# Units of 512, 384 and 256 tokens, batch 0 transposed on TensorE, and the later loads on the GpSimd queue, in an attention and channel-mix kernel

## The chip, the cores and the metric

One core of one Trainium2 chip. The time is the device time of a run in microseconds (us). Most executions of one kernel agree within 0.3%; a run over 1.5% above the fastest of its kernel is called slow here, and only fast runs are compared. Before: 229.57 us, median of 3 (228.76 to 230.91); with a fourth run in the comparison below, 229.41.

Engines: PE is TensorE's matmul, PEld its weight load, DVE is VectorE, ACT is ScalarE, POOL is GpSimd, SP is SyncE. A trailing q ("SPq") is an engine's sequencer. SyncE only issues DMAs here.

## The reference, cut to what matters

Eight batches, eight heads, 576 tokens, head size 64. The attention is linear, so it costs little; the channel mix after it has the arithmetic.

```python
q_s = softmax(q, axis=-1)          # over the 64 of a head
k_s = softmax(k, axis=2)           # over the 576 tokens
kv  = einsum('bhsd,bhse->bhde', k_s, v)
x   = einsum('bhsd,bhde->bhse', q_s, kv)      # -> (8, 576, 512)

x_prev = x shifted by one token
xk = mu_k * x + (1 - mu_k) * x_prev
xr = mu_r * x + (1 - mu_r) * x_prev
k  = maximum(xk @ w_k, 0)          # 512 -> 1024
v  = k * k @ w_v                   # 1024 -> 512
out = sigmoid(xr @ w_r) * v
```

## The kernel before

Each batch is done in two groups of four heads. `attention(b, g)` is a generator: ACT makes exp(q), exp(k) and a bf16 copy of v; VectorE normalises q into `qs`; PE makes `kvp`; a DMA transpose turns `qs` into `qt`; PE multiplies it by `w` into `xp`; ACT and VectorE make `xb`, `xd`, and the mixed `xk` and `xr`. `unit(n)` is the channel mix of 384 tokens: 8 `kfp` groups of four matmuls (`xk @ w_k`), then for each 128 tokens one `rp` (`xr @ w_r`) and one `vp` (the squares times `w_v`). The program interleaves steps of the attention of a later batch with the pieces of a unit.

```python
    def emit_load(b: int, g: int, gate=None):
        t = ldpool.tile([128, 3, 2, J * D], F32, tag="raw", name="raw")
        for i, src in enumerate((q, k, v)):
            ap = ...                                  # 128 partitions x 2 rows of 2304 bytes
            ld = nc.sync.dma_start(out=t[:, i, :, :], in_=ap)
            after(ld, gate)                           # a semaphore wait, where given
            gate = None
        ...
    # in attention():
        qt = apool.tile([128, J, 128], BF16, tag="qt", name="qt")
        nc.sync.dma_start_transpose(out=qt[:], in_=qs[:].rearrange("p j c -> p (j c)"))
    # in unit(): each 128 tokens of the result are two stores
                nc.sync.dma_start(out=dst, in_=ot[64 * i:64 * i + 64, :])
    # weights: ten DMAs with a cast to bf16, all issued by nc.gpsimd, behind batch 0's first v load
    wdone = emit_weights(first)
    ...
    emit_load(1, 0, wdone[3])         # batch 1's loads wait for weights
    emit_load(1, 1, wdone[7])
    ...
                if b + 1 < B:         # later: the loads of the next batch
                    emit_load(b + 1, g, wdone[-1] if b == 1 and g == 0 else None)
                yield from attention(b, g)
```

So SyncE issues every load of q, k and v, every transpose and every store; GpSimd issues only weights, the last of them at 17 us.

The softmax here doesn't subtract the row's maximum and nothing guards it: scores larger than these inputs give would overflow.

## Time and profile before

| what | before |
|---|---|
| time, median | 229.57 us |
| profiled span | 228.1 us |
| PE busy | 182.5 us (80%) |
| VectorE busy | 160.1 us (70%) |
| first long run of `kfp` | 42.3 us |

PE's 45.6 us of idle time (228.1 less 182.5) lie mostly in front of 42 us. The prediction shows those lines. Two more views. The first is of the tile `qt` (duration of the issue in ns as min/median/max, first and last start in us, then the time from issue to landing):

```profile
L189 SPq DMA_TRANSPOSE qt<-qs x16: 1273/1475/10114, 8.8 to 147.6; - x16
...
DMA to landing us min/median/max: 3.2/3.8/16.5
```

Fourteen of sixteen transposes behave alike, and the two of batch 0 took up to 16.5 us. The second is the queues (packets, MB, share of 16 engines' span); q1 carries what SyncE issues, q0 what GpSimd issues:

```profile
q1 hardware_dynamic: 37760, 42.48, 66.8%
q0 software_dynamic: 2208, 2.62, 6.7%
```

### The profile page before, as it was taken

The page shows a single profiled execution, that of the slowest core. Times are in us where ns is not written, and L with a number is a line of the kernel's source. Part 1 is how long each engine was busy: PE and PEld are TensorE (multiplying, and loading weights), DVE is VectorE, ACT ScalarE, POOL GpSimd, SP SyncE. Part 2 cuts the span into 40 slices and gives each one's busy share as a digit, 9 for nine tenths or more (in the row PEclk, how much of TensorE's full clock was granted, in tenths as well). Part 3 has the DMA queues.
Part 4 walks back from the last instruction along what each step waited for, and adds up shares of the span by engine and source line. Part 5 has one row for each costly group of instructions (what it writes and reads, how often), then busy time and mean ns, then how long its engine had stood idle before and what let it go on. Part 6 is the DMA issues. An engine that isn't in the chain of part 4 may idle for free.

```text
span 228.1 us, 3352 instructions
## 1 busy us (share of the span) xinstructions
PE 182.5 (80%) x1153; PEld 92.8 (41%) x1169; DVE 160.1 (70%) x367; ACT 136.0 (60%) x213; POOL 7.1 (3%) x16
## 2 busy tenths in 40 slices
PE   0100055599989989979999999999999999999991
PEld 0100032254543534434544545545545454554540
DVE  0550077899989999799999999995867843343521
ACT  4544048699597886697685994946437254352720
POOL 2360000000000000000000000000000000000000
PEclk9999999599999999999999999999999999999999
DMA  6999999999799999999899899444041140414114
GB/s 222 362 318 207 195 314 393 259 334 285 171 303 295 247 318 232 279 293 275 282 264 313 248 277 275 92 93 98 3 92 46 40 101 1 111 26 95 46 46 95
DMA packets 40009, 45.32 MB, mean 199 GB/s; under 512 B 21048, under 2 KB 22584, under 8 KB 39992
## 3 DMA queue, kind: packets, MB, share of 16 engines
q1 hardware_dynamic: 37760, 42.48, 66.8%
q0 software_dynamic: 2208, 2.62, 6.7%
q8 instruction: 9, 0.15, 0.3%
q14 instruction: 8, 0.07, 0.1%
q10 hardware_dynamic: 24, 0.00, 0.0%
HBM read 33.56 MB, written 9.44 MB: 189 GB/s over the span
## 4 chain that ended last, share of the span: by engine, by line
PE 53%; DVE 18%; DMA 14%; SPq 7%; ACT 3%; issue 2%; DVEq 0%
PE vp L241 21%; PE kfp L223 19%; PE rp L234 10%; DMA raw<-in_q_dram 8%; SPq L189 5%; DMA raw<-in_k_dram 4%; DVE qs L169 3%; DVE rsum L165 3%; PE xp L194 2%; DVE xm L209 2%; DMA qt<-qs 2%; PE kvp L177 2%; DVE xd L203 2%; ACT eqk L157 2%; DVE xk L211 1%
## 5 line engine op out<-in xcount | busy, mean ns | idle before, releaser
L223 PE MATMUL kfp<-xk,wk_bf 128*128 128x384 bf16 x384 | 71.2, 336 | 7.0 <-DVE xk L211 6.4
L227 ACT ACTIVATE rel<-kfp 128x384 bf16<-128x384 f32 x96 | 45.9, 498 | 24.3 <-PE kfp L223 22.5
L223 PEld LDWEIGHTS <-wk_bf 128*128 128x128 bf16 x384 | 36.9, 100 | 34.8 <-issue 10.6
L157 ACT ACTIVATE eqk<-raw 128x1152 bf16<-128x1152 f32 x32 | 37.1, 1167 | 13.6 <-DMA raw<-in_k_dram 6.6
L244 DVE SCALAR_TENSOR_TENSOR ot<-th,vp 128x512 f32<-128x512 f32 x36 | 24.7, 685 | 23.9 <-PE vp L241 20.8
L237 ACT ACTIVATE th<-rp 128x512 f32<-128x512 f32 x36 | 21.6, 601 | 27.6 <-PE rp L234 27.1
L234 PE MATMUL rp<-wr_bf,xr 128*128 128x512 bf16 x132 | 36.5, 379 | 0.6
L194 PE MATMUL xp<-qt,w 128*128 128x512 bf16 x64 | 13.4, 306 | 18.3 <-DMA qt<-qs 17.0
L165 DVE TENSOR_REDUCE rsum<-eqk 128x18 f32<-128x1152 bf16 x16 | 21.4, 1339 | 6.8 <-ACT eqk L157 6.8
L169 DVE TENSOR_TENSOR qs<-eqk,rrec 128x1152 bf16<-128x1152 bf16 x16 | 21.7, 1354 | 0.2
L209 DVE TENSOR_SCALAR xm<-xd,mu 128x576 bf16<-128x576 bf16 x64 | 20.7, 367 | 0.1
L234 PEld LDWEIGHTS <-xr 128*128 128x128 bf16 x144 | 13.4, 98 | 14.2
L177 PEld LDWEIGHTS <-eqk 64*128 64x128 bf16 x288 | 9.4, 99 | 17.5 <-issue 9.7
L194 PEld LDWEIGHTS <-w 128*128 128x128 bf16 x64 | 5.8, 103 | 25.6 <-issue 15.5
L177 PE MATMUL kvp<-vv_100,eqk 64*128 64x129 bf16 x108 | 4.9, 232 | 10.4 <-ACT vv_100 L161 10.4
L197 ACT CAST xb_102<-xp 128x576 bf16<-128x576 f32 x12 | 7.6, 647 | 7.8 <-PE xp L194 7.8
L200 DVE COPY xb_102<-xb_102 128x126 bf16<-128x126 bf16 x6 | 1.2, 194 | 15.2 <-ACT xb_102 L197 15.2
L184 DVE SCALAR_TENSOR_TENSOR w<-kvp,rz,mask 128x128 bf16<-128x128 f32 x32 | 9.7, 342 | 0.2
L197 ACT CAST xb_110<-xp 128x576 bf16<-128x576 f32 x10 | 6.4, 639 | 4.6 <-PE xp L194 4.5
L161 ACT CAST vv_100<-raw 128x1152 bf16<-128x1152 f32 x6 | 7.0, 1167 | 1.5 <-DMA raw<-in_v_dram 1.5
L241 PE MATMUL vp<-wv_bf,k_961 128*128 128x512 bf16 x24 | 6.0, 380 | 1.7 <-DVE k_961 L229 1.7
L161 ACT CAST vv_108<-raw 128x1152 bf16<-128x1152 f32 x5 | 5.8, 1161 | 2.3 <-DMA raw<-in_v_dram 2.3
(75 smaller groups left out, 198.2 us busy)
## 6 DMA issues: line engine op xcount, KB each, us to landing
raw<-in_q_dram SPq DMA_DIRECT2D x16, 576.0 KB, 5.6
raw<-in_k_dram SPq DMA_DIRECT2D x16, 576.0 KB, 5.4
raw<-in_v_dram SPq DMA_DIRECT2D x16, 576.0 KB, 8.3
out_dram<-ot SPq DMA_DIRECT2D x72, 128.0 KB, 2.5
wk_bf<-in_moe_w_k_dram POOLq DMA_DIRECT2D x4, 256.0 KB, 7.6
wv_bf<-in_moe_w_v_dram POOLq DMA_DIRECT2D x2, 512.0 KB, 14.5
wr_bf<-in_moe_w_r_dram POOLq DMA_DIRECT2D x4, 128.0 KB, 11.1
qt<-qs SPq DMA_TRANSPOSE x16, 3.8
```

The costliest lines, as they stand in the source:

```text
L157: nc.scalar.activation(out=eqk[:, i, :, :, :], in_=t[:, i, :, :].rearrange("p u (j d) -> p j u d", d=D), func=ACT.Exp)
L165: nc.vector.reduce_sum(out=rsum[:], in_=eq, axis=AX.X)
L169: nc.vector.tensor_tensor(out=qs[:].rearrange("p j (u d) -> p (j u) d", u=2), in0=eq, in1=rrec[:, :, None].to_broadcast((128, 2 * J, D)), ...
L177: nc.tensor.matmul(kvp[:, hf, 0:129], lhsT=eqk[r, 1, j, :, :].rearrange("p u d -> p (u d)"), rhs=vv[r, j, 0:129], start=(j == 0), stop=(j ...
L194: nc.tensor.matmul(xp[:, 64 * c:64 * e], lhsT=w[:, hf, :], rhs=qt[:, c:e, 64 * hf:64 * hf + 64], start=True, stop=True)
L209: nc.vector.tensor_scalar(out=xm[:, hf, :], in0=xd[:, hf, :], scalar1=mu[:, c:c + 1], scalar2=None, op0=ALU.mult)
L223: nc.tensor.matmul(kfp[:, 0:U], lhsT=wk_bf[:, ct, fc * 128:(fc + 1) * 128], rhs=xk[:, ct, c0:c0 + U], start=(ct == 0), stop=(ct == CT - 1))
L227: nc.scalar.activation(out=rel[:], in_=kfp[:, 0:U], func=ACT.Relu, scale=HALF_ROOT)
L234: nc.tensor.matmul(rp[:], lhsT=xr[:, ct, c0 + 128 * m:c0 + 128 * m + 128], rhs=wr_bf[:, ct, :], start=(ct == 0), stop=(ct == CT - 1))
L237: nc.scalar.activation(out=th[:], in_=rp[:], func=ACT.Tanh, scale=0.5)
L241: nc.tensor.matmul(vp[:], lhsT=k2[:, ft, 128 * m:128 * m + 128], rhs=wv_bf[:, ft, :], start=(ft == 0), stop=(ft == FT - 1))
L244: nc.vector.scalar_tensor_tensor(out=ot[:], in0=th[:], scalar=1.0, in1=vp[:], op0=ALU.add, op1=ALU.mult)
```

## The change

Its intent: start the channel mix earlier (no DMA transpose for batch 0), spread the attention's work evenly over the units, and keep the loads from waiting behind transposes by giving them a queue of their own. The gates that held batch 1's and batch 2's loads until weights had landed go with it. The diff, cut to its core:

```diff
-    U = 384
-    NU = B * S // U
+    UNITS = ((0, 512), (512, 384), (896, 256))
...
-    def emit_load(b: int, g: int, gate=None):
+    def emit_load(b: int, g: int, queue):
...
-            ld = nc.sync.dma_start(out=t[:, i, :, :], in_=ap)
-            after(ld, gate)
-            gate = None
+            ld.append(queue.dma_start(out=t[:, i, :, :], in_=ap))
...
-    first = emit_load(0, 0)
-    emit_load(0, 1)
+    emit_load(0, 0, nc.sync)
+    first = emit_load(0, 1, nc.sync)[0]
...
-        nc.sync.dma_start_transpose(out=qt[:], in_=qs[:].rearrange("p j c -> p (j c)"))
+        if b == 0:
+            qtp = psum.tile([128, 16, 128], BF16, tag="att", bufs=2, name="qtp")
+            for j in range(J):
+                nc.tensor.transpose(out=qtp[:, j, :], in_=qs[:, j, :], identity=ident[:])
+            nc.scalar.copy(out=qt[:], in_=qtp[:, 0:J, :])
+        else:
+            nc.sync.dma_start_transpose(out=qt[:], in_=qs[:].rearrange("p j c -> p (j c)"))
...
-    emit_load(1, 0, wdone[3])
-    emit_load(1, 1, wdone[7])
+    emit_load(1, 0, nc.gpsimd)
+    emit_load(1, 1, nc.gpsimd)
...
-                    emit_load(b + 1, g, wdone[-1] if b == 1 and g == 0 else None)
+                    emit_load(b + 1, g, nc.gpsimd)
...
-            goal = min((B - 1) * ASTEPS, ASTEPS + int(ASTEPS * n / 1.5) + 1)
...
+                cols += c
+                advance(min((B - 1) * ASTEPS, ASTEPS * (cols + per_batch // 8) // per_batch))
```

The last lines are the pacing: before, the steps of attention ran ahead by units and were done at about 181 us (the last `xr`); now they follow the columns of PE work, an eighth of a batch ahead.

More of the change, by code (lines that the diff above doesn't have):

```diff
@@ L46 @@
     FT = F // 128
-    U = 384
-    NU = B * S // U
-    assert B % 2 == 0 and (2 * S) % U == 0
+    UNITS = ((0, 512), (512, 384), (896, 256))
+    assert B % 2 == 0
     const = ctx.enter_context(tc.tile_pool(name="const", bufs=1))
@@ L66, in after @@
             tc.add_manual_dep(later.ins, earlier.ins.name, SYNC)
-    def emit_load(b: int, g: int, gate=None):
+    def emit_load(b: int, g: int, queue):
         t = ldpool.tile([128, 3, 2, J * D], F32, tag="raw", name="raw")
+        ld = []
         for i, src in enumerate((q, k, v)):
@@ L213, in attention, with unit @@
             yield
-    def unit(n: int):
-        xk, xr = xpair[n // 3]
-        c0 = U * (n % 3)
-        k2 = mpool.tile([128, FT, U], BF16, tag="k2", name="k2")
+    def unit(pair: int, c0: int, n: int):
+        xk, xr = xpair[pair]
+        k2 = mpool.tile([128, FT, 512], BF16, tag="k2", name="k2")
         for fc in range(FT):
@@ L222, in unit @@
             for ct in range(CT):
-                nc.tensor.matmul(kfp[:, 0:U], lhsT=wk_bf[:, ct, fc * 128:(fc + 1) * 128],
-                                 rhs=xk[:, ct, c0:c0 + U],
+                nc.tensor.matmul(kfp[:, 0:n], lhsT=wk_bf[:, ct, fc * 128:(fc + 1) * 128],
+                                 rhs=xk[:, ct, c0:c0 + n],
                                  start=(ct == 0), stop=(ct == CT - 1))
-            rel = mpool.tile([128, U], BF16, tag="rel", bufs=3, name="rel")
-            nc.scalar.activation(out=rel[:], in_=kfp[:, 0:U], func=ACT.Relu,
+            rel = mpool.tile([128, 512], BF16, tag="rel", bufs=3, name="rel")
+            nc.scalar.activation(out=rel[:, 0:n], in_=kfp[:, 0:n], func=ACT.Relu,
                                  scale=HALF_ROOT)
-            nc.vector.tensor_tensor(out=k2[:, fc, :], in0=rel[:], in1=rel[:], op=ALU.mult)
-            yield
-        for m in range(U // 128):
+            nc.vector.tensor_tensor(out=k2[:, fc, 0:n], in0=rel[:, 0:n], in1=rel[:, 0:n],
+                                    op=ALU.mult)
+            yield n
+        for m in range(n // 128):
             rp = psum.tile([128, C], F32, tag="mm", bufs=4, name="rp")
@@ L237, in unit @@
             nc.scalar.activation(out=th[:], in_=rp[:], func=ACT.Tanh, scale=0.5)
-            yield
+            yield 512
             vp = psum.tile([128, C], F32, tag="mm", bufs=4, name="vp")
@@ L246, in unit @@
             for i in range(2):
-                jb = (U * n + 128 * m) // 64 + i
+                jb = (2 * S * pair + c0 + 128 * m) // 64 + i
                 bb, j = jb // J, jb % J
@@ L251, in unit @@
                 nc.sync.dma_start(out=dst, in_=ot[64 * i:64 * i + 64, :])
-            yield
+            yield 1024
     def drain(gen):
@@ L256, in drain @@
             pass
-    wdone = emit_weights(first)
+    emit_weights(first)
     a0 = attention(0, 0)
@@ L273, in attention_of, with advance @@
                 if b + 1 < B:
-                    emit_load(b + 1, g, wdone[-1] if b == 1 and g == 0 else None)
+                    emit_load(b + 1, g, nc.gpsimd)
                 yield from attention(b, g)
-    ASTEPS = 16
-    MSTEPS = 14
+    ASTEPS = 14
     att = attention_of(range(1, B))
     done = 0
-    for n in range(NU):
-        goal0 = done
-        if n == 0:
-            goal = ASTEPS
-        else:
-            goal = min((B - 1) * ASTEPS, ASTEPS + int(ASTEPS * n / 1.5) + 1)
-        for i, _ in enumerate(unit(n)):
-            want = goal0 + (goal - goal0) * (i + 1) // MSTEPS
-            while done < want:
-                next(att, None)
-                done += 1
+    cols = 0
+    per_batch = S * (FT + CT * 3)
+    def advance(want):
+        nonlocal done
+        while done < want:
+            next(att, None)
+            done += 1
+    for pair in range(B // 2):
+        for c0, n in UNITS:
+            advance(ASTEPS * (2 * pair + (c0 + n - 1) // S))
+            for c in unit(pair, c0, n):
+                cols += c
+                advance(min((B - 1) * ASTEPS, ASTEPS * (cols + per_batch // 8) // per_batch))
     drain(att)
```

## The prediction

> **What bounds the kernel now.** I read the page first, then the chain of waits, the times by stretch, the timeline of the first 50 us and the groups by line. The page gives the split:
>
> ```profile
> PE 182.5 (80%) x1153; PEld 92.8 (41%) x1169; DVE 160.1 (70%) x367; ACT 136.0 (60%) x213; POOL 7.1 (3%) x16
> PE   0100055599989989979999999999999999999991
> DVE  0550077899989999799999999995867843343521
> DMA  6999999999799999999899899444041140414114
> ```
>
> PE has the most work, but the idle is not spread over the span: PE is all but blank for five slices of 5.7 us, half busy for three, and nearly full after that. VectorE is nearly full from the eighth slice to the 27th and then half empty, so its work comes early. The stretches give numbers (columns: span, busy time and count per engine, granted clock, DMA share, GB/s):
>
> ```profile
> 16.00:24.00 8.00, 0.00 (x0) 0.00 (x0) 0.00 (x0) 2.32 (x2) 0.75 (x1) 1.00 1.19 215
> 24.00:28.00 4.00, 0.00 (x0) 0.00 (x0) 0.00 (x0) 0.00 (x0) 0.00 (x0) 1.00 1.22 194
> 36.00:40.00 4.00, 1.08 (x20) 0.71 (x19) 2.75 (x5) 3.94 (x5) 0.00 (x0) 0.95 1.07 395
> 42.00:44.00 2.00, 1.67 (x6) 0.81 (x6) 1.66 (x6) 0.69 (x2) 0.00 (x0) 0.50 1.16 184
> ...
> 60.00:120.00 60.00, 54.68 (x355) 27.17 (x361) 57.51 (x130) 45.56 (x73) 0.00 (x0) 1.00 1.00 277
> 160.00:215.00 55.00, 54.79 (x318) 28.47 (x321) 29.66 (x72) 25.57 (x50) 0.00 (x0) 1.00 0.25 58
> ```
>
> From 16 to 28 us PE and VectorE do nothing at all while the DMA engines are full, at only about 200 GB/s; from 60 to 120 us VectorE is 96% busy and PE loses 5.3 us; from 160 us PE is alone and loses 0.2 in 55. The chain in order of time says what the early hole is (start, length, what):
>
> ```profile
> 2.26 8.41 DMA raw<-in_q_dram
> ...
> 13.72 1.27 DVE qs L169
> 14.99 0.27 DVE w L184
> 15.26 9.87 SPq L189
> ...
> 26.88 9.15 DMA raw<-in_q_dram
> ...
> 41.61 0.68 DVE xk L211
> 42.29 0.04 issue
> 42.33 4.00 PE kfp L223 x12
> ```
>
> L189 is the DMA transpose of batch 0. It holds SyncE's queue 9.87 us, the q load behind it is issued only at 26.88 and lands at 36.0, and the channel mix starts in earnest at 42.33 us. The waits agree:
>
> ```profile
> PE xp L194 <- DMA qt<-qs: 17.0, 2, 16.2
> ```
>
> **PE's floor.** Steady spacing from the chain: 32 kfp in 5.20 us, 4 rp in 0.86, 8 vp in 1.73, 18 kvp in 0.63, 4 xp in 0.65. So 96 kfp groups of 4 are 62.4, 36 rp 31.1, 36 vp 62.3, 16 kvp 10.1, 16 xp 10.4: 176.3 us at full clock. The 228.1 us span is that plus about 37 us net before 42.33 (42.33 less 5 us of useful PE work: four kvp, about half the xp of two groups, eight kfp), 2 us of half clock (the twelve kfp in 4.00 us take 333 ns each, against 163 later), 7 us of later idle, and 5 us after the last matmul (the last vp ends at 223.1; then ot of 0.69, the store, the end).
>
> **What the Trainium skill says.** "DMA: Bandwidth & Descriptors", section "Issuing engines are not separate DMA queues": queues of different engines run on the same 16 DMA engines, and another issuer saves only sequencer time. So a GpSimd queue buys no bandwidth; here the sequencer time is large (9.87 us), because the transpose blocks the loads behind it. "TensorE: Matmul & The Clock Gate", "Part 1: The HAM clock gate (the "warmup" mystery)": two clock states, half after an idle window of about 3.4 us. The trace agrees: 0.50 from 40 to 46 us after idle, then 1.00. "Part 4: PE-mode transpose" of that page: a full 128x128 transpose on TensorE goes to PSUM and needs a copy after; no transpose of that kind is in this trace. "SBUF — State Buffer", "SBUF: two separate sides": a DMA from GpSimd has its descriptors written over a port pair that VectorE's 2-port modes lock. In the trace GpSimd's ten weight issues took 0.60 to 0.83 us and the 1.35 us VectorE operations beside them kept their length, but few of the fast bf16 ones fell there, so it shows neither.
>
> **The change part by part.**
>
> 1. Batch 0 on PE. Removed: two DMA transposes that landed after up to 16.5 us. Added: 18 PE transposes of 128 columns, about 0.06 us warm and 0.11 cold by columns (163 ns for 384, doubled cold), so 1 to 2 us of PE, and two ACT copies of 128x1152, which at the 1.16 us of the casts of that shape are 2.3 us. I follow the chain with before's durations. qs of group 0 is ready at 8.75, v has landed at 9.2 and is cast by 10.4, kvp is done by 12 and w by 13.8. ACT meanwhile does q and k of group 1 (to 13) and its v (to about 14.2), so the first qt copy ends near 15.4. Then xp 0.8, two xb copies of 0.65, and group 0 is mixed by 19. Group 1 takes turns on the two "att" PSUM buffers: kvp 16.3 to 17.2, transposes to 18, copy 19.1, xp to 20, xb 20.7, then boundary copy, xd, two xm, xk (0.2 + 0.75 + 0.56 + 0.67): **xk complete at about 22.8 us**, where before it was 42.3. A few kfp halves go ahead of it, so the effective start is 21.
>
> 2. Loads and weights. With no transposes in the way I take 375 GB/s of HBM read (36 to 40 us showed 395 moved). Batch 0 is 3.54 MB, weights 5.24, batch 1 3.54. Landing: batch 0 about 12.5, wk about 16, wv about 26, batch 1 about 35 to 37. vp of the first unit is not due before 21 + 7 = 28, so weights hide. Batch 1's q load, now behind the weights on GpSimd, should land earlier than the 36.0 of before, and all of the batch, which was later than that, with it.
>
> 3. First unit of 512. Its PE work is 32 x 0.216 + 4 x 0.865 + 4 x 1.73 = 17.3 us, all of batch 0, against 13.0 for 384. That covers 21 to 38.3, plus 2 cold and 2.6 of batch 1's kvp and xp: 43. Batch 1's x needs VectorE: per batch about 15.1 us of instruction times (group: 1.34 + 0.26 + 1.35 + 0.17 + 0.68 + 0.19 + 0.75 + 1.3 + 1.5), 13.6 after overlap (the groups add to 178, busy is 160). From q's landing at about 31 that, with four ot of 0.69, gives 47. So PE meets a **hole of 3 to 4 us at 43 to 47**, the new wait.
>
> 4. Unit sizes later. Columns are unchanged, and the pieces scale: PE, relu and squares per pair of batches stay equal. No gain, no loss of more than 1 us; the 256-wide matmul (108 ns) is near the 98 ns of a weight load, but these overlap.
>
> 5. Pacing. Attention is spread evenly, an eighth of a batch ahead, over all units, not squeezed into the first 165 us. VectorE per batch is 160/8 = 20 us against PE's 22: 91%, where before it was 96% from 60 to 120. This should save a part of the 5.3 us lost there. But the last steps of a batch are emitted just at the end of a 512 unit, and the next unit needs that xk: ot, xd, xm, xk are 2.6 us, less 1.3 of kfp on the channels already there. About 1.3 us at each of four pairs. I count 5 us of steady loss, against 7.
>
> The sum: 176.3 + 1.5 transposes + 17.3 start (21 less 3.7 useful) + 2 half clock + 3.5 hole + 5 steady + 5 tail = 210.6 us of span. The measured time of the profiled run was 1.7 above its span (229.83 against 228.1), so about **211 to 212; I put 211**.
>
> **Rivals.** (a) VectorE takes over. For: 91% average, 96% within a 512 unit that also carries a batch's attention (13.6 + 5.5 of 19.9 us). Against: before, PE still ran 91% at 96% VectorE. If each pair loses 4 us: 218 or more. (b) GpSimd's queue starves: descriptors in software, 42 loads of perhaps 0.7 us beside fast VectorE operations, or VectorE held up by them. At 0.3 us on each of 42 it is 13 us of VectorE, of which the slack takes much: 214 to 220. Against: no such stretching in the overlap that before has. (c) Batch 1 still lands late because weights go first in one queue; the start gain is then paid at the first batch boundary: each us late is a us. If it lands at 42: 217. (d) Better: the hole vanishes and steady loss falls to 2: 204. (e) No gain, if the front were hidden anyway: PE's blank 16 to 28 us and 99% density at the end speak against it; all time saved in front comes out at the end.
>
> **Range and chances.** Front gain 17 to 22 us, hole 0 to 8, steady loss 2 to 10 give 204 to 219; eight in ten in 205 to 218. Faster by over 2% (below 225) needs only a quarter of the front gain: 0.95. Within 2% 0.04, slower 0.01.
>
> **What will show it.** Step 1: first xp near 15 to 16 us, first long kfp run near 21 to 23, and no wait of PE on qt in the start. Step 2: the idle of ACT on raw loads small; batch 1's v landed by 37; DMA above 300 GB/s from 8 to 35 us. Step 3: PE idle of 3 to 4 us on xk between 40 and 48. Step 5: VectorE about nine tenths till near 200 us, PE idle before kfp on xk at pair boundaries of 1 to 2 us. The prediction is wrong if GpSimd's loads land much later than 37, if VectorE's fast operations get longer than before's 0.75 and 0.32 us, or if the clock halves again in the hole.

## The result

The changed kernel took **241.74 us** (median of 4, 239.01 to 246.35), against 229.41 (228.76 to 230.91). Two of the four are slow runs; the fast ones took 239.01 and 240.02. The ratio is 1.043, with a 95% interval of 1.034 to 1.053: slower by 4%. All ratios here are the mean time of one kernel's fast runs over that of the other's fast runs of the same rounds, so not quite the ratio of the medians. The output was correct. The prediction of 211 us was wrong, also in direction.

The first profile of the changed kernel fell in a slow run (243.46 us), so the same kernel was run again, as the first experiment:

> The changed kernel once more, for a second profile beside the others of this chip. Theory R (rings): the DMA transposes of the later batches, on SyncE's ring, take turns packet by packet with the loads that now stand in GpSimd's ring; about 1334 small packets each, 83 on each of 16 engines, against load packets of 4 KB (0.18 us at 370 GB/s over 16 engines), so up to 83 x 0.18 = 15 us. It expects landings of 10 to 17 us again where many loads are queued, holes of all engines at about 40 us and 60 us, and 239 to 247 us. Theory P (pacing and unit sizes lose the time) and theory V (GpSimd's descriptor work slows VectorE) expect the same time but no such landings as the cause.

It took 241.01 us (238.98 to 245.4, 4 runs, two of them slow; the fast ones 238.98 and 239.37), ratio 1.041 (1.038 to 1.044), and its profile is of a fast run: 237.6 us of span. All lines "of the changed kernel" below are from it. Its page first, as tenths of busy time in 40 slices of 5.9 us, and the queues:

```profile
span 237.6 us, 3409 instructions
...
PE   0077591049096789999999999999999999999992
...
PEclk9999799559959999999999999999999999999998
DMA  6999999935994999999999799225416030231313
...
q0 software_dynamic: 8256, 27.40, 38.8%
q1 hardware_dynamic: 23968, 17.11, 32.8%
```

PE does start earlier: the third and fourth slice are at 7, where before they were at 0. Then the seventh and eighth are at 1 and 0, where before they were at 5, and the eleventh is at 0, where before it was at 9. GpSimd's queue now takes 38.8% of the DMA engines' time. The stretches (columns: span, busy time and count of PE, PEld, DVE, ACT, POOL, granted clock, DMA share, GB/s):

```profile
28.00:38.00 10.00, 8.79 (x49) 3.63 (x47) 8.07 (x16) 8.71 (x13) 4.34 (x6) 0.86 1.03 390
38.00:50.00 12.00, 0.00 (x0) 0.00 (x0) 0.66 (x2) 0.00 (x0) 0.72 (x1) 0.62 0.99 351
50.00:60.00 10.00, 8.87 (x48) 3.65 (x48) 6.12 (x14) 7.32 (x9) 2.17 (x3) 0.77 0.37 108
60.00:120.00 60.00, 49.20 (x302) 24.12 (x303) 48.63 (x100) 39.68 (x62) 14.78 (x21) 0.94 1.02 265
```

From 38 to 50 us PE and ACT do nothing and VectorE has two instructions, while the DMA engines are full. After it the clock is 0.77 for 10 us. From 60 to 120 us PE does 49.2 us where before it did 54.7. The chain in order of time (start, length, what) names the hole:

```profile
32.82 1.08 ACT vv L159
33.90 16.76 DMA qt<-qs
50.79 1.12 PE xp L198 x4
...
56.86 8.86 DMA qt<-qs
...
75.47 8.37 DMA qt<-qs
...
134.42 11.09 DMA out_dram<-ot
```

It is the first DMA transpose, of batch 1 now: 2.1 us of issue on SyncE, 1.9 more until its first packet at 37.9, and 12.2 of transfer. From 36.8 us on PE stands at `xp`, the next matmul in its order; behind it wait five `vp` matmuls whose squares VectorE had made by 36.8 us, and which run at once when `xp` is through. Two more transposes follow, and at 134 us a store that lands after 11 us. PE's waits for `qt` (us in total, times, longest), which before were 17.0 in two, and the tile's view, which before read 3.2/3.8/16.5:

```profile
PE xp L198 <- DMA qt<-qs: 22.4, 3, 14.0
...
DMA to landing us min/median/max: 3.2/7.5/13.5
```

The whole median has doubled, where before only two transposes were long.

The account by stretches closes. PE's idle time is the span less its busy time: 45.6 us before, 48.0 after. In the pieces, 16 to 38 us gained 10.1 us (idle 15.9 before, 5.9 after), then 38 to 50 lost 8.1, 50 to 60 lost 0.9, and 60 to 120 lost 5.5; all other stretches together gained 2.0. Busy time rose by 7.1 us (182.5 to 189.6), of which the 18 PE transposes are 2.3; most of the rest is put down to matmuls at half clock. That is an estimate: the trace has half clock at 27 to 31, 41 to 55 and 65 to 72 us with 12.7 us of PE work in it, half of which would be extra, and before at 40 to 46 us with 4.1; so about 4 of the 4.8 us. Idle and busy together: 2.4 + 7.1 = 9.5 us, the growth of the span.

Two of the prediction's own tests pass. VectorE's fast operations were to get longer if GpSimd's issues held them up (groups of the changed kernel: busy us, mean ns, idle before):

```profile
L213 DVE TENSOR_SCALAR xm<-xd,mu 128x576 bf16<-128x576 bf16 x64 | 21.2, 373 | 0.3
...
L207 DVE TENSOR_TENSOR xd<-xb 128x1152 bf16<-128x1152 bf16 x16 | 12.1, 753 | 0.4
```

The means before were 367 and 745 to 748 ns: 1 to 2% longer, half a microsecond in all. And the loads do not land late: ACT has cast the last of batch 1's first group at 34.0 us, when the transpose is issued. At this place everything was on time but the transpose.

### What the DMA engines did in the hole

The trace records each packet of each DMA engine. I counted them by kind. One transpose of `qs` is 1,152 packets of 256 bytes, 72 on each of 16 engines, 18 ns each in the median. A load issued on SyncE or ACT is in packets of 2,304 bytes, about 93 ns; the same load issued on GpSimd is in packets of 4,608 bytes, about 187 ns. While the first transpose of the changed kernel ran:

```
us from start      transpose packets   load packets (4608 B, 188 ns)
42                        95                 80
43                        90                 82
44                        97                 81
45                        89                 78
```

Nearly one for one. The loads move 80 x 4,608 bytes a microsecond in the mean of the four, 370 GB/s; the transpose gets 93 x 256, 24 GB/s. The sum works out: in the 12.2 us from its first packet to its last, 860 load packets passed, 54 on each engine; 54 x 188 ns = 10.1 us, and 72 x 18 ns = 1.3 us for the transpose itself: 11.4. The transpose is not slow, it takes turns with packets ten times as long as its own.

That gave the **theory (T)**: the DMA engines alternate between queues packet by packet, so a transpose alone in SyncE's queue takes one turn against each long load packet of GpSimd's queue. With the loads in the same queue they would be ahead of it or behind it, not in turns with it. Rivals: **(G)** GpSimd's issuing or its descriptors are slow in themselves; **(P)** the new units and pacing lose the time; **(O)** the compiler's order of instructions moved by chance. The expectations call T "R" or "rings" (rings are what this text calls queues), G in part "S" (the software queue as such), and "V" is the prediction's rival that GpSimd's issues slow VectorE. The 1,334 packets and 83 turns in the first of them counted every packet under 512 bytes; the transposes' own are 1,152 and 72.

T is about the first hole. The second and third transpose of the chain show it only in part: their packets took 4.2 and 4.0 us beside 126 and 120 load packets, and of the 8.9 and 8.4 us in the chain 3.4 and 3.8 are SyncE's issue.

### The profile page after: what moved, and what is told of

Same layout as the page of the kernel before. It is cut to its first block, busy times and chain, and to the rows that moved or that the text cites. A ratio compares the mean times of both kernels' runs of the same rounds, so it can differ in the third digit from the quotient of the medians.

```text
span 241.7 us, 3392 instructions
## 1 busy us (share of the span) xinstructions
PE 190.9 (79%) x1170; PEld 96.4 (40%) x1187; DVE 165.3 (68%) x367; ACT 135.8 (56%) x215; POOL 37.4 (15%) x58
## 3 DMA queue, kind: packets, MB, share of 16 engines
q0 software_dynamic: 8256, 27.40, 38.8%
## 4 chain that ended last, share of the span: by engine, by line
PE 44%; DMA 25%; DVE 19%; ACT 7%; issue 2%; SPq 1%; DVEq 0%; ACTq 0%
PE vp L245 18%; PE kfp L226 14%; DMA qt<-qs 10%; DMA out_dram<-ot 10%; PE rp L238 8%; DMA raw<-in_k_dram 4%; DVE qs L167 3%; DVE rsum L163 3%; PE xp L198 3%; DVE xm L213 2%; DVE ot L248 2%; DVE xd L207 2%; PE kvp L175 2%; DVE xk L215 2%; ACT eqk L155 1%
## 5 line engine op out<-in xcount | busy, mean ns | idle before, releaser
L226 PE MATMUL kfp<-xk,wk_bf 128*128 128x384 bf16 (+2 forms) x380 | 73.6, 343 | 10.8 <-DVE xk L215 7.1
L230 ACT ACTIVATE rel<-kfp 128x512 bf16<-128x512 f32 (+2 forms) x96 | 44.7, 498 | 32.8 <-PE kfp L226 27.6
L226 PEld LDWEIGHTS <-wk_bf 128*128 128x128 bf16 x384 | 37.6, 102 | 39.6 <-issue 18.2
L238 PE MATMUL rp<-wr_bf,xr 128*128 128x512 bf16 x135 | 37.6, 388 | 0.5
L198 PE MATMUL xp<-qt,w 128*128 128x512 bf16 x64 | 14.8, 320 | 22.3 <-DMA qt<-qs 19.4
L74 POOL DMA_DIRECT2D raw<-in_q_dram x14 | 10.2, 728 | 82.7 <-ACT vv_100 L159 32.4
L213 DVE TENSOR_SCALAR xm<-xd,mu 128x576 bf16<-128x576 bf16 x64 | 21.4, 377 | 0.3
L238 PEld LDWEIGHTS <-xr 128*128 128x128 bf16 x144 | 13.7, 101 | 15.8 <-issue 2.0
L198 PEld LDWEIGHTS <-w 128*128 128x128 bf16 x64 | 6.3, 105 | 30.7 <-issue 22.5
L74 POOL DMA_DIRECT2D raw<-in_k_dram x14 | 10.1, 725 | 3.4 <-DMA wv_bf<-in_moe_w_v_dram 2.2
L74 POOL DMA_DIRECT2D raw<-in_v_dram x14 | 10.1, 724 | 2.5 <-DMA raw<-in_q_dram 2.5
## 6 DMA issues: line engine op xcount, KB each, us to landing
raw<-in_k_dram POOLq DMA_DIRECT2D x14, 576.0 KB, 10.7
```

What stands on the lines that cost most here:

```text
L74: ld.append(queue.dma_start(out=t[:, i, :, :], in_=ap))
L198: nc.tensor.matmul(xp[:, 64 * c:64 * e], lhsT=w[:, hf, :], rhs=qt[:, c:e, 64 * hf:64 * hf + 64], start=True, stop=True)
L213: nc.vector.tensor_scalar(out=xm[:, hf, :], in0=xd[:, hf, :], scalar1=mu[:, c:c + 1], scalar2=None, op0=ALU.mult)
L226: nc.tensor.matmul(kfp[:, 0:n], lhsT=wk_bf[:, ct, fc * 128:(fc + 1) * 128], rhs=xk[:, ct, c0:c0 + n], start=(ct == 0), stop=(ct == CT - 1))
L230: nc.scalar.activation(out=rel[:, 0:n], in_=kfp[:, 0:n], func=ACT.Relu, scale=HALF_ROOT)
L238: nc.tensor.matmul(rp[:], lhsT=xr[:, ct, c0 + 128 * m:c0 + 128 * m + 128], rhs=wr_bf[:, ct, :], start=(ct == 0), stop=(ct == CT - 1))
```

## The experiments

All gave correct results. Times are medians of all runs, slow ones too, with the range and number of runs (4 where none is given); ratios are of fast runs alone. Of the four runs with loads on ACT three are slow, and no ratio was recorded.

| run | time, us | ratio to before |
|---|---|---|
| changed kernel again | 241.01 (238.98 to 245.4, 4) | 1.041 (1.038 to 1.044) |
| changed, loads back on SyncE | 220.34 (219.8 to 222.71, 4) | 0.961 (0.955 to 0.966) |
| before, loads on GpSimd | 260.66 (257.37 to 262.37, 4) | 1.137 (1.129 to 1.144) |
| changed, loads on ACT | 285.59 (280.73 to 287.65) | none |
| changed, padded load tiles | 240.22 (238.0 to 241.86) | 1.043 (1.036 to 1.050) |
| changed, all transposes on PE | 220.98 (220.64 to 221.42) | 0.962 (0.957 to 0.966) |
| loads on SyncE, batches 0 and 1 on PE | 219.03 (218.4 to 220.24) | 0.954 (0.950 to 0.959) |
| changed, loads wait for the transpose | 236.76 (236.4 to 237.08) | 1.031 (1.027 to 1.035) |
| batch 1's loads on GpSimd, later on SyncE, 0 and 1 on PE | 220.62 (220.35 to 222.12) | 0.961 (0.956 to 0.965) |
| before, only batch 0 on PE | 225.77 (225.28 to 227.65) | 0.983 (0.978 to 0.988) |
| before, only units and pacing | 225.18 (224.96 to 225.4) | 0.979 (0.975 to 0.982) |
| changed, batches 0 and 1 on PE | 232.73 (227.66 to 244.74, 20) | 0.997 (0.995 to 1.000) |
| mixed and gated | **216.02 (215.62 to 216.35, 4)** | **0.941 (0.937 to 0.944)** |
| mixed and gated, only batch 0 on PE | 222.62 (221.78 to 224.2) | 0.970 (0.965 to 0.975) |

### Undo one part: the loads back on SyncE

```diff
-    emit_load(1, 0, nc.gpsimd)
+    emit_load(1, 0, nc.sync)          # and in the two other places
```

> The changed kernel with one part undone: loads of batches 1 to 7 on SyncE's queue again, the rest kept (transposes of batch 0 on PE, units, pacing, weights on GpSimd). R: transposes land in 3 to 5 us, behind loads of their own ring in order rather than in turns, no hole at 40 us, 208 to 216 us. P: still 235 or more. V: about 230 or less too, but with VectorE's instruction means 1 to 3% shorter as the only change.

220.34 us: between fast runs one word in three places is worth 19 us (239.2 against 220.3), and turns the change into a gain of 4%. The weights' gates stay dropped. The time missed the expected 208 to 216, and a hole is left, which T had not expected. The landings of `qt`, and that hole in the chain:

```profile
DMA to landing us min/median/max: 3.7/4.6/8.1
```

```profile
28.04 13.57 DMA qt<-qs
```

Once the first transpose's packets start, they are done in 2.5 us: at 40 us the trace counts 644 transpose packets in one microsecond, beside 46 of loads. The 13.57 us of this chain are another thing: 9.1 us of issue, in which the packets of SyncE's queue are all of loads, 77 to 97 a microsecond, in turns with 81 to 96 of weights from GpSimd's queue. The transpose stands behind them. PE waits for `qt` 4.0 us here, once. So the part to blame is found; T and G are both left.

### Do that part alone: before, with its loads on GpSimd

```diff
-            ld = nc.sync.dma_start(out=t[:, i, :, :], in_=ap)
+            ld = queue.dma_start(out=t[:, i, :, :], in_=ap)   # nc.gpsimd from batch 1 on, no gates
```

> The kernel before with that part alone: loads of batches 1 to 7 on GpSimd's queue after the weights, transposes of batch 0 still by DMA. R: transposes up to 15 us or more, several of them, and 235 to 255 us, slower than before by over 2%. P: as before, 229 within 2%. V: slower, with VectorE's means longer by 3% or more and transposes at 4 us.

260.66 us, 13.7% slower, and worse than the 235 to 255 that I had expected. The median landing of `qt` went from 3.8 to 7.1 us and PE's waits for it from 17.0 us to 37.0, but the longest landing was 8.7, not 15 or more. In the kernel before, the part (the queue, and the gates that go) costs 28 us by the two fast runs, 31 by the medians; in the changed one 19. P cannot explain either.

### GpSimd, or a second queue? The loads on ACT

```diff
-    emit_load(1, 0, nc.gpsimd)
+    emit_load(1, 0, nc.scalar)        # and in the two other places
```

> The changed kernel with the loads of batches 1 to 7 on ACT's hardware queue instead of GpSimd's software one: again another ring than the transposes', but packets of one 2304-byte row instead of 4 KB. R: turns of 0.10 us, so the slowest transposes land after about 83 x 0.10 = 8 us, between the two others, and the time lies between theirs, 215 to 232 us. Theory S (it is the software queue as such): transposes at 3 to 5 us, 208 to 216 us. ACT's own work may be delayed by its 42 issues of 0.5 us.

The time missed by far: 285.59 us against an expected 215 to 232. PE waited for `qt` nine times, 36.7 us in all, though the packets of ten of the fourteen transposes passed in 1.6 to 3.2 us. PE's order of instructions is also far from the changed kernel's: compared by operation, source line and tile, 485 lines of difference over some 2,400 rows, where the run with the loads on SyncE has 161. So the time can't be put down to queues, and what it is due to stays open. Its packets do speak of queues, and the landing of `qt` at most 8.3 us was as expected ("about 8"):

```
first transpose of batch 1      loads on    load packets beside it    first to last packet
changed kernel, again           GpSimd      860 of 4608 B, 188 ns           12.2 us
this run                        ACT         905 of 2304 B,  94 ns            7.8 us
loads back on SyncE             SyncE        87 of 2304 B                    2.5 us
```

With the loads in ACT's queue a transpose still takes turns with them: 168, 153, 171 and 154 of its packets in four successive microseconds, beside 154, 149, 153 and 150 of loads. One for one, and 1.7 times as many turns a microsecond, since the other packet is half as long. So it is not GpSimd as an engine (G falls for the turn-taking): the second queue that was tried does it too, and the length of its packets sets the price.

### Halve GpSimd's packets

```diff
-        t = ldpool.tile([128, 3, 2, J * D], F32, tag="raw", name="raw")
+        t = ldpool.tile([128, 3, 2, J * D + 16], F32, tag="raw", name="raw")   # rows no longer adjoin
```

> The changed kernel with 64 bytes of padding after each 2304-byte row of the load buffer, so that the two rows of a head pair no longer lie side by side and a GpSimd load is written in packets of 2304 bytes, not 4608. The order of instructions on every engine is the same as in the changed kernel. Theory R (turns by packet between the two rings): about 850 load packets of 93 ns instead of 186 pass within the first transpose, so its packets take 850 x 0.093 / 16 + 1.3 = 6 to 8 us, not 12, the hole at 39 us shrinks by about 5 us and the time is 230 to 237 us. If the rings share by bytes, or if software descriptors are what is slow, the first transpose stays at 12 us or grows and the time stays at 239 us or more.

The experiment missed its purpose. The trace still shows 4,608-byte packets, 845 of them beside the first transpose, which took 12.5 us; the time was 240.22. A gap between the two rows in SBUF does not split GpSimd's packet. It is a repeat of the changed kernel with the same order of instructions, and nothing more.

### No DMA transposes at all

```diff
-        if b == 0:
+        if True:
```

> The changed kernel with all batches transposed on PE: no DMA transpose at all, loads still on GpSimd. PE gets 14 x 9 x 0.056 = 7 us more, ACT 14 x 1.1 = 15 us more. R: no hole at 40 us, stores land in under 5 us, 212 to 222 us. If GpSimd's queue itself is the trouble (late loads, or VectorE held up), holes remain before the exponentials and the time is 230 us or more.

220.98 us, as expected, with all loads on GpSimd. No hole: PE is busy 21.9 of the 25 us from 25 to 50, and the DMA engines move about 400 GB/s from 25 to 70 us. So loads on GpSimd's queue leave no hole where no transpose meets them (against G once more). PE pays for the 144 transposes: busy 192.7 us.

### Keep the loads on GpSimd, but behind the transpose

```diff
-            nc.sync.dma_start_transpose(out=qt[:], ...)
+            tr = nc.sync.dma_start_transpose(out=qt[:], ...)
+            if b + 1 < B:
+                after(emit_load(b + 1, g, nc.gpsimd)[0], tr)
```

> The changed kernel, loads on GpSimd, but each load of batches 2 to 7 waits until the transpose of the same half of the batch before has landed, so that far fewer loads stand in GpSimd's ring beside a transpose. R: at most three loads beside a transpose (384 packets of 186 ns over 16 engines, 4.5 us), so transposes take 2 to 6 us, the first hole 5 us or less, 214 to 226 us. If GpSimd's queue as such is slow, 235 or more.

236.76 us, not the 214 to 226 that I had expected of T. The first step went as it should: 54 load packets beside the first transpose, 3.1 us from its first packet to its last. But the waits and the chain of this kernel show what took its place:

```profile
POOL raw L74 <- DMA qt<-qs: 104.3, 11, 14.3
```

```profile
33.77 4.89 DMA qt<-qs
...
73.36 11.67 DMA raw<-in_v_dram
...
107.53 10.95 DMA out_dram<-ot
```

The 12 us hole is gone (4.89), and the loads, which now wait 104 us in total for transposes, come late at 73 us. Two later transposes still met loads, and stores too, and took 8.5 and 9.6 us. They had only 239 and 225 load packets beside them, about 15 on each engine; turns of the usual 187 ns explain 3 us of each, and the rest is the long packets of "What stays open" below. The store that took 10.95 us to land stands in SyncE's queue behind such a transpose. By the letter of the expectation, 235 or more speaks for G; what speaks against it are the run without DMA transposes and the packets of the run on ACT.

### Is it the transposes of batch 1 alone?

```diff
-        if b == 0:
+        if b <= 1:          # on the changed kernel: loads all on GpSimd
```

> The changed kernel with batch 1 also transposed on PE, all later loads still on GpSimd. R: the 12 us hole at 39 us goes, the later transposes (from about 50 us) still take turns with loads and up to 10 us: 224 to 234 us, between the changed kernel (239) and the one with all transposes on PE (221).

232.73 us over 20 runs, from 227.66 to 244.74; the seven that count as fast have a median of 229.1. As expected, and by the fast runs as long as the kernel before. The first hole is avoided, but the first DMA transpose, later now, took 14.5 us beside 1,055 load packets.

Now the same kernel with the loads of batches 2 to 7 on SyncE; batch 1's stay on GpSimd, when no DMA transpose is about:

```diff
-                    emit_load(b + 1, g, nc.gpsimd)
+                    emit_load(b + 1, g, nc.sync)
```

> A version meant to beat both: batches 0 and 1 transposed on PE, the loads of batch 1 on GpSimd behind the weights, all later loads on SyncE in one ring with the DMA transposes. R: the front runs as with all transposes on PE (steady kfp from 27 to 28 us), and later transposes take 2 to 3 us of packets as in the runs with loads on SyncE: 211 to 216 us. If it stays at 219 or more, the front of the earlier version was not what held it.

220.62 us, not the 211 to 216 that I had expected. But this pair tests O: the order of instructions is nearly the same in both (34 lines of difference over PE's 2,415 rows), and the time differs by 8.5 us, fast runs against fast runs. Chance order is not the cause of that. What it missed by is in its chain:

```profile
26.86 16.07 DMA raw<-in_v_dram
```

Batch 2's loads, which wait for nothing, are in SyncE's queue at once, and until about 30 us take turns with the weights in GpSimd's (177 packets of them in 2 us beside 176). Batch 1's loads stand behind the weights and pass only from 32 us on. What is needed first loses half of the turns to what is not needed yet. A third kernel had shown the same: batches 0 and 1 on PE, every load on SyncE.

```diff
-        if b == 0:
+        if b <= 1:
...
-    emit_load(1, 0, nc.gpsimd)
+    emit_load(1, 0, nc.sync)          # and in the two other places
```

> Loads of all batches on SyncE, and batches 0 and 1 transposed on PE, the rest of the change kept. The run with the loads on SyncE still lost 28 to 42 us behind the first DMA transpose, which stood in the ring behind loads. R: with none in that time the hole goes, 209 to 215 us, faster than that run by 5 to 10 us. If something else than the transpose starves the front, no more than 3 us gained, 217 or more.

219.03 us against an expected 209 to 215: batch 1's loads on SyncE took turns with the weights on GpSimd, its v landed at 32.4 us, and the steady `kfp` began at about 35. By these two runs the turn-taking also costs between plain transfers, if one of them is needed first; the next run tests it.

### Mixed and gated

So the remedy is to let nothing into the second queue before it is wanted: batch 2's first load waits for batch 1's last.

```diff
+    ready = emit_load(1, 1, nc.gpsimd)[-1]
...
+                    ld = emit_load(b + 1, g, nc.sync)[0]
+                    if b == 1:
+                        after(ld, ready)
```

> The mixed version (batches 0 and 1 transposed on PE, batch 1 loaded on GpSimd behind the weights, later loads on SyncE), with the loads of batch 2 held until batch 1 has landed. In the mixed version they stood in SyncE's ring from the start and took turns with the weights: wr landed after 10.9 us and batch 1's v after 16.1. R, applied to loads against loads: without that, steady kfp from 27 to 28 us as with all transposes on PE, and 211 to 216 us, which was my predicted time. If it stays at 219 or more, turns between rings do not explain what was left, and my sum was wrong elsewhere.

**216.02 us**, 6% faster than before, just at the end of what I had expected (211 to 216), and all four runs within 0.8 us. Against the mixed version the gate alone is worth 4.6 us. The page's row of PE, one stretch and the start of the channel mix:

```profile
PE   0056689989999999798999999999999999999990
```

```profile
60.00:120.00 60.00, 57.21 (x379) 29.84 (x385) 55.04 (x123) 44.92 (x74) 0.00 (x0) 1.00 1.00 272
```

```profile
27.50 7.03 PE L226 MATMUL kfp<-xk,wk_bf 128*128 128x512 bf16 x24 [2.52 <-DMA wv_bf<-in_moe_w_v_dram]
```

The row has no digit under 5 after the first two slices and before the last, and 60 to 120 us holds 57.2 us of PE where the changed kernel had 49.2. No DMA transpose meets a load of another queue.

The same with batch 1's transposes as DMAs:

```diff
-        if b <= 1:
+        if b == 0:
```

> The same, with batch 1 transposed by DMA again, so that it differs from the changed kernel only in where and when batches 2 to 7 are loaded. R: beside batch 1's first transpose only the rest of batch 1 is in GpSimd's ring (at most three loads, 384 packets, 4.5 us), so 3 to 7 us for it, less for the rest, 212 to 219 us. If the changed kernel's order of instructions was at fault and not the rings, 230 or more.

222.62 us, 3.6 beyond the end of what I had expected (212 to 219), but far from the 230 or more of O: it differs from the changed kernel only in where and when batches 2 to 7 are loaded, and is 17 us faster (fast runs). Its first transpose was short, 3.0 us with 16 load packets beside it, as T says. But PE was busy only 5.2 of the 10 us from 50 to 60, waiting for a second one and for VectorE's mixing after it. At this place the DMA transpose is on the path, short or not.

### The other two parts alone

Before, with only the transposes of batch 0 on PE, and loads and gates as they were:

```diff
-        nc.sync.dma_start_transpose(out=qt[:], ...)
+        if b == 0:
+            ...                       # the nine PE transposes and the ACT copy, as in the change
+        else:
+            nc.sync.dma_start_transpose(out=qt[:], ...)
```

> The kernel before with the first part alone: the two DMA transposes of batch 0 replaced by PE transposes and ACT copies. My step 1 expects the channel mix to begin about 15 us earlier and 212 to 220 us. If the front is held by something else (weights, the gated loads of batch 1), less than 5 us gained, 225 or more.

225.77 us: a gain of 1.7% (1.2 to 2.2), much less than expected (212 to 220). The chain shows what takes the removed wait's place:

```profile
16.44 16.81 DMA wv_bf<-in_moe_w_v_dram
```

The steady `kfp` begins at 32.5 us, 10 earlier than before, but SyncE waits 13.9 us for weights before it issues batch 1's first q load, at 20.4, and 9.5 more, until 33.3, before batch 2's. So the two parts seem to need each other: the early start is only worth something if batch 1 follows. No run has this kernel without the gates, so that is argued.

Before, with only the units of 512, 384, 256 and the even pacing:

```diff
-    U = 384
+    UNITS = ((0, 512), (512, 384), (896, 256))
...                                    # unit(pair, c0, n) and the pacing loop, as in the change
```

> The kernel before with the units of 512, 384 and 256 tokens and the even pacing alone. My steps 3 to 5 expect 2 to 4 us from the longer first unit and the steadier VectorE: 224 to 229 us. Theory P (units and pacing lose the time) expects 232 us or more.

225.18 us, a gain of 2.1% (1.8 to 2.5), as expected: P falls. The stretch from 80 to 200 us, first of the kernel before, then of this one:

```profile
80.00:200.00 120.00, 115.69 (x734) 58.85 (x743) 98.36 (x227) 76.43 (x129) 0.00 (x0) 1.00 0.66 178
```

```profile
80.00:200.00 120.00, 118.81 (x763) 60.49 (x773) 103.20 (x233) 78.78 (x136) 0.00 (x0) 1.00 0.65 180
```

PE loses 1.2 us in 120 where it lost 4.3.

## Why the prediction was wrong

**The step that failed is step 2, with the assumption beside it that a DMA transpose goes on landing in 3.8 us.** Step 3 shows the gap: its path goes from q's landing at 31 us over VectorE's time to x at 47, with no transpose in it. "So a GpSimd queue buys no bandwidth", I wrote, and took the queue for neutral in everything but sequencer time. The share that a transpose gets while another queue is full was never asked. The runs put in its place: with a full second queue the transpose gets one of its 256-byte packets for each 4,608-byte one, 12.2 us in place of 2.5. Undone, 220.3 us in place of 239.2 (fast runs); done alone, 1.137 of before.

**The same thing was on the page before, and I misread it.** The 9.87 us of SyncE at 15.26 I called a transpose that "blocks the loads behind it". By the packets, batch 0's first transpose took 8.5 us beside 1,136 packets of weights from GpSimd's queue (71 on each engine beside its own 72, most of them 1,024 bytes and 96 ns), and the second 3.9 us beside 470. It was the taking of turns already; before its first packet, at 18.5 us, the transpose stood behind loads of its own queue. A maximum of 16.5 beside a median of 3.8 us asked for a reason; I gave one that made the cure look free.

**Step 1** had the right direction and the wrong size. The first `xp` came as predicted: 15.8 us in the changed kernel, against 15 to 16. The steady `kfp` came at 27.7, not at 21 to 23:

```profile
15.77 0.64 PE L198 MATMUL xp<-qt,w 128*128 128x512 bf16 x2 [1.40 <-ACT qt L191]
...
20.99 1.44 PE L226 MATMUL kfp<-xk,wk_bf 128*128 128x512 bf16 x3 [1.40 <-DVE xk L215]
22.22 0.69 PE L198 MATMUL xp<-qt,w 128*128 128x512 bf16 x2
```

Two matmuls of `xp` take 0.64 us at half clock, nine transposes 1.14, and three `kfp` of group 0 sit between the halves of group 1's `xp`, which feed the `xk` that everything waits for. Group 1's q also landed at 12.0 us, later than the 10.7 of before. The term "17.3 us of start" was, by an estimate from these starts, about 5 us too small.

**Step 2's landing times** were, taken alone, good: ACT had batch 1's first group cast by 33.9 us. Rival (c), late loads, is not in the changed kernel; it came in two of my own experiments, with the loads on SyncE beside weights on GpSimd.

**Step 3**, a hole of 3 to 4 us on `xk`, did not come where the transposes were out of the way: in the mixed and gated kernel PE is busy 21.1 of the 22 us from 28 to 50. The changed kernel has a hole of 12 us at nearly the same place, for the other reason.

**Step 4**: nothing in the runs speaks of a cost of the sizes, but no run has the sizes without the pacing. **Step 5** was right and better than I put it, though its "first 165 us" should be 181: 1.2 us lost from 80 to 200 with sizes and pacing alone and 0.7 in the changed kernel with its loads on SyncE, where before it was 4.3; the mixed and gated kernel, which runs earlier in the same stretch, lost 3.1.

**Rivals.** (a), VectorE takes over, and (b), GpSimd and VectorE hold each other up, are refuted: VectorE's operations kept their length, and with the loads moved alone the kernel was 220.3 us, with VectorE as before. None of my five rivals was the true one, and the chance of 0.01 for slower had no ground: the change put new traffic beside the DMA that was on the path, and no rival looked there. The last clause of the prediction's own test, "if the clock halves again in the hole", did come true.

Does the rest of the sum hold? The run that only puts the loads back on SyncE, 220.3 us, is still above the predicted range of 205 to 218. The mixed and gated kernel, at 216.0, lies in it, but it also has batch 1 on PE and a gate, and there two errors partly cancel: the start came about 5 us late and the hole of 3.5 us did not come. That is in part luck. The sum itself slips too: 210.6 and 1.7 are 212.3, not 211.

**What stays open.** Between 100 and 148 us of the changed kernel some transposes took 5 to 10 us though only about 200 load packets passed beside them. The median packet there was as long as ever (loads 180 ns, transposes 18), but 65 of 1,520 load packets took over 1 us, up to 2.8. In the mixed and gated kernel 7 of 3,558 did, and no transpose took over 3 us. Transposes of 5 us or more beside loads from batch 1 on are seen only in kernels with the loads and the transposes in two queues; I have no run that explains the long packets. So the turns are shown for the first hole, and for the whole of the 19 us they are not. The scatter of those kernels (239 to 247 us, and 228 to 245) is as little explained.

**The skill.** The Trainium skill, "DMA: Bandwidth & Descriptors", section "Queues, rings and completion order", states that each DMA engine round-robins between the queue rows that it has work for, packet by packet. The trace agrees, 93 packets against 80 in a microsecond, if what it records as packets are the page's. I had read the page and drawn on another section of it, "Issuing engines are not separate DMA queues", by which another issuer only saves sequencer time. That holds for the total rate (390 GB/s in the stretch from 28 to 38 us), but not for the time of one transfer: 12.2 us against 2.5 for the first transpose.

## What to carry to other kernels

Before you give one kind of DMA a queue of its own, ask which transfer is on the path, how long its packets are, and whose packets it will alternate with: here a transfer in small packets starved beside a full queue of large ones (12.2 us), while in one queue with them it waited once behind them and then passed in 2.5. In a kernel like this one, keep such transfers in the queue of the loads, keep the other queues empty while they run, and gate loads that are not needed yet. Where a DMA's longest latency is far above its median (16.5 and 3.8 us here), count packets before explaining it.

## What the Trainium skill lacked or had wrong

- "DMA: Bandwidth & Descriptors", "Issuing engines are not separate DMA queues", says that DMAs of different engines interleave and that issuing on several engines only saves issue time. Here the issuer of the loads alone moved the kernel from 220.3 to 239.2 us, and in another pair from 220.6 to 229.1 (fast runs); a sentence should point to the arbitration between queues and its effect on small packets.
- The same page does not say in how many packets a DMA transpose goes. Here one of 128x1152 bf16 was 1,152 packets of 256 bytes at 18 ns, 72 on each engine, and beside a queue of 4,608-byte packets it got 24 GB/s against their 370.
- The same page, "Queues, rings and completion order", describes the turns but not what they cost: 2.5 us for a transpose beside 87 load packets, 7.8 beside 905 of 2,304 bytes, 12.2 beside 860 of 4,608.
- The same page, "Rules for kernel authors", says "A transpose next to ordinary DMAs needs nothing", in a row on wrong results. For results that held in every run; for time it did not (a first transpose from 2.5 to 14.5 us).
- No page that I found says that the same load has packets of 4,608 bytes from GpSimd and of 2,304 from SyncE or ACT, and that a gap between the two rows in SBUF does not change the former.
- "SBUF — State Buffer", "SBUF: two separate sides", warns of VectorE and GpSimd holding each other up when GpSimd issues DMAs. With 42 such loads VectorE's fast operations went from 367 to 373 and from about 746 to 753 ns: nothing to speak of in this kernel.
